# Staging q and k halves in place, one tile form for P times V, and another order of products in the middle experts of an attention, expert and gated-layer kernel

## The chip, the cores and the metric

The kernel runs on one core of a Trainium2 chip. The metric is the device time of one execution in microseconds (us), smaller is better. Times come from repeated executions; one further execution is profiled, and its trace is what the rows below are read from. The engines are TensorE (PE, with its weight loads as PEld), VectorE (DVE), ScalarE (ACT), GpSimd (POOL) and SyncE (SP), which issues most of the transfers.

## The reference

Three layers follow one another: attention with a threshold, a layer of eight experts with one expert for each token, and a gated layer.

```python
# q, k, v: (2, 8, 576, 64)
scores = scale * q @ k.T
thresh = max(scores) - tau
scores = where(scores >= thresh, scores, -1e9) - max(scores)
attn = exp(scores); attn /= sum(attn) + 1e-9
x = (attn @ v)                       # -> 1152 tokens x 512
# experts: w1 (8, 512, 1024), w2 (8, 1024, 512), capacity 288
expert_idx = argmax(x @ w_gate);  gate_w = softmax(x @ w_gate)[expert_idx]
y = relu(x_e @ w1[e]) @ w2[e]        # tokens of expert e
x = gate_w * y                       # 0 where over capacity
# gated layer: w_gate, w_val (512, 1536), w_out (1536, 512)
out = (silu(x @ w_gate) * (x @ w_val)) @ w_out
```

## The kernel before

All products keep float32 accuracy by halves: an operand is rounded to a shorter form (hi), the rest is subtracted (lo), and hi*hi + lo*hi + hi*lo are added up in PSUM.

**Attention.** Four head pairs (hp) of nine units each: four query tiles of batch 0, four of batch 1, and one unit for the tails (576 = 512 + 64). A unit (two heads) is four score products of 288 columns for the two heads (eight in the tail unit), the maximum, exponential and threshold on VectorE and ScalarE, nine transposes of the result e (L653), and, in batches, P times V (L675 for the 128-row blocks, L678 for the 64-row tail, on the V tail `vt`) and the x tasks (L709). The order on TensorE is written out by hand, by credits and by the unit numbers TST, QST and UST. Units count from 0, so hp 1 ends with unit 17 and hp 2 begins with unit 18.

The key tile KP of a head holds hi in one half of the partitions and lo in the other, so that one product multiplies both by a query tile. For each next head pair `stage_tasks` does the following: TensorE transposes raw k and q (L515), ScalarE copies the result out (L528, L530), GpSimd rounds it (L508) and subtracts (L510) on 128 partitions, which hold both heads, and SP's transfers rearrange the four quarters (head by hi or lo) into KP and the query tiles (L537 for k, L540 for q, L559 for the key tails, L568 for the query tails). Those are 28 transfers for a head pair, in the order k of batch 0, q of batch 0, tails, k of batch 1, q of batch 1.

**Experts.** Routing sorts the tokens; the experts come by size, in windows of 128, 128, 128, 144, 176, 192, 224 and 224 tokens. The first three go through `expert_rows`, which the change leaves alone. The others go through `expert`: eight h tiles (`ps_h`, first product), then four output tiles (`ps_y`, second product) of eight h tiles each. `mm_win` makes each product of two instructions: one of 2W columns (hi and lo of the tokens side by side, L1231) and one of W columns (L1232); `total` then adds the two halves of the result (a copy on ScalarE, L1240, and an addition on VectorE, L1241), and VectorE makes h's lo half (L1358). The two widest experts take their second weights in halves.

**Gated layer.** Gate and value products (L1460) and the output product (L1507 to L1509). The change leaves it alone.

## Time and profile before

| | |
|---|---|
| three runs | 566.77, 564.54, 561.7 us; median 564.54 |
| profiled execution | 564.97 us, span 563.3, mean granted clock 0.986 |
| TensorE, weight loads | 536.4 us (95%), 481.0 (85%) |
| VectorE, ScalarE | 409.7 us (73%), 295.2 (52%) |
| GpSimd | 85.4 us (15%) |
| attention | 0 to some 172 us |
| routing | 172 to 185 us |
| eight experts | 185 to 332 us |
| gated layer | 332 us to the end |

Busy time is the time in which an engine executes; weight loads run beside TensorE's products. The granted clock is the share of TensorE's full clock of 2.4 GHz that it was given, and has two levels, so a value between 0.5 and 1.0 over a stretch is a mix of 1.2 and 2.4 GHz.

### The profile page before, as it was taken

What the parts mean: (1) busy time and instruction counts of PE and PEld (TensorE: products, weight loads), DVE (VectorE), ACT (ScalarE), POOL (GpSimd) and SP (SyncE); (2) the same over time, 40 slices, a digit from 0 to 9 for tenths busy, and PEclk for the clock granted to TensorE, in tenths of its full rate; (3) what the DMA queues carried; (4) which work ended last, traced back from release to release, by engine and by line L of the source; (5) the groups of instructions that cost most, each with busy time, mean ns of one, the idle gap of its engine ahead of it and who ended that gap; (6) DMA issues with size and microseconds to landing.
All of it is one profiled execution on the core that took longest, in us unless ns stands there. A gap on an engine that the chain in (4) does not pass through costs nothing. (4 is left out here: it accounts for less than half of the span.)

```text
span 563.3 us, 9844 instructions
## 1 busy us (share of the span) xinstructions
PE 536.4 (95%) x3600; PEld 481.0 (85%) x3602; DVE 409.7 (73%) x825; ACT 295.2 (52%) x573; POOL 85.4 (15%) x145
## 2 busy tenths in 40 slices
PE   7999988999997799999999999999999999999996
PEld 6787866877773799998998889999999999888884
DVE  5988876888876399989988977888896748722220
ACT  4977664676651399877866743334332333332321
POOL 6541050055452500000000000000000000011101
PEclk8999998999999799999999999999999999999999
DMA  7557467457301888977666442442341300000001
GB/s 185 173 150 171 118 143 172 110 140 205 116 29 35 313 289 281 328 224 232 224 219 223 151 149 81 145 149 83 143 149 76 112 40 1 0 38 37 20 38 42
DMA packets 67895, 77.94 MB, mean 138 GB/s; under 512 B 25216, under 2 KB 43136, under 8 KB 67840
## 3 DMA queue, kind: packets, MB, share of 16 engines
q1 hardware_dynamic: 66256, 72.52, 42.4%
q0 software_dynamic: 1440, 4.72, 2.2%
q8 instruction: 30, 0.49, 0.3%
q14 instruction: 25, 0.20, 0.1%
q10 hardware_dynamic: 144, 0.00, 0.0%
HBM read 61.89 MB, written 4.72 MB: 118 GB/s over the span
## 5 line engine op out<-in xcount | busy, mean ns | idle before, releaser
L1460 PE MATMUL pgv<-yT,ring 128*128 128x384 f32 x828 | 145.1, 337 | 0.0
L1460 PEld LDWEIGHTS pgv<-yT,ring 128*128 128x128 f32 x828 | 144.9, 188 | 0.0
L210 ACT CAST ring<-raw 128x1024 fp32r<-128x1024 f32 x57 | 60.8, 1066 | 51.2 <-DVE raw L238 49.5
L657 ACT COPY pT<-ps_pt 128x512 f32<-128x512 f32 (+1 forms) x108 | 52.3, 486 | 41.6 <-PE ps_pt L653 41.6
L607 DVE TENSOR_REDUCE nm<-s 128x1 f32<-128x576 f32 x72 | 54.4, 755 | 17.2 <-PE s L597 17.1
L631 DVE SCALAR_TENSOR_TENSOR e<-s,th,e 128x576 f32<-128x576 f32 x72 | 58.7, 816 | 6.2 <-ACT e L620 4.9
L1513 POOL DMA_INDIRECT out_dram<-ob,ids x9 | 8.7, 972 | 358.9 <-ACT ob L1512 351.7
L620 ACT ACTIVATE e<-s,nm 128x576 f32<-128x576 f32 x72 | 54.3, 754 | 2.2 <-DVE nm L607 1.8
L288 DVE TENSOR_TENSOR ring<-raw,ring 128x1024 fp32r<-128x1024 f32 x44 | 53.3, 1218 | 0.0
L1231 PE MATMUL ps_y<-h,ring 128*128 128x448 f32 (+3 forms) x160 | 48.8, 370 | 3.6 <-DVE h L1358 3.4
L214 DVE TENSOR_TENSOR hs<-h,hs 128x768 fp32r<-128x768 f32 x18 | 17.2, 958 | 48.1 <-ACT hs L210 48.1
L653 PE MATMUL ps_pt<-ident,e 128*128 128x128 f32 x324 | 47.9, 276 | 0.0
L1231 PE MATMUL ps_h<-xw,ring 128*128 128x448 f32 (+3 forms) x160 | 46.4, 362 | 0.0
L1508 PE MATMUL po<-ring,hs 128*128 128x512 f32 x108 | 42.0, 389 | 0.0
L1507 PE MATMUL po<-ring,hs 128*128 128x512 f32 x108 | 42.0, 389 | 0.0
L1509 PE MATMUL po<-ring,hs 128*128 128x512 f32 x108 | 42.0, 389 | 0.0
L1232 PE MATMUL ps_y<-h,ring 128*128 128x224 f32 (+3 forms) x160 | 40.0, 250 | 0.0
L1232 PE MATMUL ps_h<-xw,ring 128*128 128x224 f32 (+3 forms) x160 | 40.0, 250 | 0.0
L675 PE MATMUL ps_pv<-pT,v 128*64 128x256 f32 (+2 forms) x400 | 39.9, 331 | 0.0
L653 PEld LDWEIGHTS ps_pt<-ident,e 128*128 128x128 f32 x324 | 39.7, 142 | 0.2 <-issue 0.2
L1231 PEld LDWEIGHTS ps_y<-h,ring 128*128 128x128 f32 x160 | 30.0, 188 | 8.3 <-DVE h L1358 7.4
L1480 ACT ACTIVATE sg<-pgv 128x384 f32<-128x384 f32 x36 | 17.5, 486 | 28.4 <-PE pgv L1460 18.9
(224 smaller groups left out, 975.9 us busy)
## 6 DMA issues: line engine op xcount, KB each, us to landing
raw<-in_moe_w_dram SPq DMA_DIRECT2D x25, 1024.0 KB, 5.1
rawx<-in_moe_w_dram SPq DMA_DIRECT2D x7, 1024.0 KB, 5.9
raw<-in_moe_w_gate_dram SPq DMA_DIRECT2D x6, 1024.0 KB, 5.0
qhl<-ring SPq DMA_DIRECT2D x16, 256.0 KB, 4.4
raw<-in_moe_w_out_dram SPq DMA_DIRECT2D x4, 1024.0 KB, 4.9
kp<-ring SPq DMA_DIRECT2D x24, 128.0 KB, 2.3
rawx<-in_moe_w_val_dram SPq DMA_DIRECT2D x3, 1024.0 KB, 5.0
raw<-in_moe_w_val_dram SPq DMA_DIRECT2D x3, 1024.0 KB, 5.0
```

The source lines that it names most:

```text
L210: nc.scalar.copy(dst, src)
L288: lo_eng.tensor_tensor(out=lo_, in0=src, in1=f32(hi_), op=ALU.subtract)
L607: nc.vector.tensor_reduce(out=nm_t[u][:, j:j + 1], in_=s_t[i][:, :, 0:SH], axis=AX.XY, op=ALU.max, negate=True)
L620: nc.scalar.activation(out=e_t[u][:, j].rearrange("p (a s) -> p a s", a=2), in_=s_t[i][:, :, 0:SH], func=ACTF.Exp, bias=nm_t[u][:, j:j + 1 ...
L631: nc.vector.scalar_tensor_tensor(out=ev, in0=s_t.pop(i)[:, :, 0:SH], scalar=th_t[u][:, j:j + 1], in1=ev, op0=ALU.is_ge, op1=ALU.mult, accu ...
L653: nc.tensor.transpose(ps[:, c * 128:(c + 1) * 128], ef[:, (c0 + c) * 128:(c0 + c + 1) * 128], ident)
L657: return lambda: nc.scalar.copy(pT[g][:, c0:c0 + m, o:o + 128], ps[:, 0:m * 128].rearrange("p (c t) -> p c t", c=m))
L1231: mm(ps[:, 0:2 * W], ws(wp, 0), x[:, 0:2 * W], start=first, stop=False)
L1232: mm(ps[:, 0:W], ws(wp, 1), x[:, 0:W], start=False, stop=last)
L1460: mm(ps[:, 0:TH], (gw, vw)[w][:, i, kk, fl * 128:(fl + 1) * 128], yT[:, x, kk, th * TH:(th + 1) * TH], start=i + x + kk == 0, stop=i == 1 ...
L1507: mm(po, hs[:, 0, fl], ws[:, 0, sl], start=f == 0, stop=False)
L1508: mm(po, hs[:, 0, fl], ws[:, 1, sl], start=False, stop=False)
```

## The change

- **Staging.** Each of GpSimd's operations works on the 64 partitions of one head and writes the half that is already on the right partitions straight into KP or the query tile; the other half goes there by one transfer. There are twice as many of these operations and 12 transfers for a head pair instead of 28. The order is k of batch 0, tails, q of batch 0, k of batch 1, q of batch 1; the constants TST and UST start the transposes and the staging one unit earlier. Raw k and q are loaded with one transfer for each batch instead of two, and V of the head pairs from 2 on is loaded five units later than before.
- **V tails.** Two persistent tiles, zeros outside the tail, so that the tail's product takes all 128 contraction rows.
- **Wide experts.** From 2W > 400 on (width 224), three products of W columns take the place of the two, and nothing is to be added behind them.
- **Widths 144, 176, 192.** The second product begins output tile 0 with six h tiles, then tile 1 with six, then adds the last two to each.
- Late constants are loaded at unit 11 instead of 5, a memset of the routing goes from VectorE to GpSimd, and the `olo` tiles share a buffer with the attention's e.

```diff
-    TST = 4
+    TST = 3
+    VST = 5
-    UST = 5
+    UST = 4
...
+    vtail = [ld.tile([128, B, 2, D], F32, name=f"vtail{i}") for i in range(2)]
...
         def main(nm, b, eng):
             if hp and nm != "v":
-                for h in range(2):
-                    eng.dma_start(r[nm][:, b, :, h],
-                                  srcs[nm][0][b, h0 + h, 0:SM, :].rearrange("(p c) d -> p c d", c=C4))
+                eng.dma_start(r[nm][:, b],
+                              srcs[nm][0][b, h0:h0 + 2, 0:SM, :].rearrange(
+                                  "h (p c) d -> p c h d", c=C4))
                 return
...
+        if hp < 2:
+            values()
+        else:
+            vlate[hp] = values
...
     def stage_tasks(hp):
...
-                    parts([x[:, i, cs] for i in range(2)], dst)
-                    for j in range(2):
-                        for i in range(2):
-                            to, frm = slice(i * D, (i + 1) * D), slice(j * D, (j + 1) * D)
-                            if nm == "k":
-                                o = ST if j else 0
-                                nc.sync.dma_start(f32(KP[hp, j][to, b, o:o + SM]), f32(x[frm, i, cs]))
-                            else:
-                                t = ring[3 + j] if hp % 2 == 0 else qhl[j]
-                                nc.sync.dma_start(f32(t[to, :, cs]), f32(x[frm, :, cs]))
+                    lo_, up = slice(0, D), slice(D, 2 * D)
+                    if nm == "k":
+                        k0, k1 = [KP[hp, j][:, b, o:o + SM] for j, o in ((0, 0), (1, ST))]
+                        x = kx[:, cs]
+                        rounded(k0[lo_], dst[lo_])
+                        rest_of(x[lo_], dst[lo_], k0[lo_])
+                        nc.sync.dma_start(f32(k0[up]), f32(x[lo_]))
+                        rounded(x[up], dst[up])
+                        rest_of(k1[up], dst[up], x[up])
+                        nc.sync.dma_start(f32(k1[lo_]), f32(x[up]))
+                    else:
+                        for j, frm, to in ((0, lo_, up), (1, up, lo_)):
+                            t = by_batch(ring[3 + j] if hp % 2 == 0 else qhl[j])[:, b]
+                            rounded(t[frm, 0:SM], dst[frm])
+                            rest_of(t[frm, SM:2 * SM], dst[frm], t[frm, 0:SM])
+                            nc.sync.dma_start(f32(t[to]), f32(t[frm]))
...
-        return [main("k", 0), main("q", 0), tails, main("k", 1), main("q", 1)], qtails
+        return [main("k", 0), tails, main("q", 0), main("k", 1), main("q", 1)], qtails
...
-                        mm(ps[j * D:(j + 1) * D, o:o + w], r["vt"][j * ST:(j + 1) * ST, bb, :],
-                           p[j * ST:(j + 1) * ST, C4, o:o + w], start=False, stop=True)
+                        mm(ps[j * D:(j + 1) * D, o:o + w], r["vt"][:, bb, j, :],
+                           p[:, C4, o:o + w], start=False, stop=True)
...
-            if 2 * W <= 512:
+            if 2 * W <= 400:
                 mm(ps[:, 0:2 * W], ws(wp, 0), x[:, 0:2 * W], start=first, stop=False)
                 mm(ps[:, 0:W], ws(wp, 1), x[:, 0:W], start=False, stop=last)
             else:
                 mm3(ps[:, 0:W], wp, ws, x, lambda x, i: x[:, i * W:(i + 1) * W], first, last)
...
+            def products(m, fs):
+                if fs[0] == 0:
+                    ps = ps8.tile([128, 512], F32, tag="m", name="ps_y")
+                    pys[m] = ps, pieces.pop(("w2", e, m))[:, :, :].rearrange(
+                        "p i (k f) -> p i k f", k=KF)
+                ps, wv = pys[m]
+                for f in fs:
+                    mm_win(W, ps, wv, lambda w, i: w[:, i, f], hs[f], f == 0, f == KF - 1)
+
+            head, tail_ = range(KF - 2), range(KF - 2, KF)
...
+                    if m == 0:
+                        products(0, head)
+                        products(1, head)
+                        products(0, tail_)
+                        products(1, tail_)
+                    elif m > 1:
+                        products(m, range(KF))
```

Three places in the order of instructions. First SP's queue and GpSimd around the staging for hp 2. SP before (`kp` key tiles, `ring_96` and `ring_95` scratch tiles, `thl` the tails, `ring_98` and `ring_99` query tiles, `xd` an output of the attention):

```order
L537 DMA kp_1118<-ring_96 64x512 x2
L537 DMA kp_1119<-ring_96 64x512 x2
L540 DMA ring_98<-ring_95 64x2x512 x2
L540 DMA ring_99<-ring_95 64x2x512 x2
L748 DMA xd<-xr 128x128
L748 DMA xd<-xr 128x2x128
L559 DMA kp_1118<-thl 64x2x64 x2
L559 DMA kp_1119<-thl 64x2x64 x2
```

SP after (`kth` is the scratch tile of the key tails):

```order
L557 DMA kp_1063<-ring_96 64x512
L560 DMA kp_1064<-ring_96 64x512
L586 DMA kp_1063<-kth 64x2x64
L589 DMA kp_1064<-kth 64x2x64
L775 DMA xd<-xr 128x128
L775 DMA xd<-xr 128x2x128
L337 DMA k<-in_k_dram 128x8x64
L566 DMA ring_98<-ring_98 64x1024
L566 DMA ring_99<-ring_99 64x1024
```

Four tail transfers stood behind eight others (k and q); now two tail transfers stand behind two, and each q tile takes one.

GpSimd before, from the first of these operations (`raw_103` holds transposed k and q):

```order
L508 TENSOR_SCALAR ring_96<-raw_103 128x512
L510 TENSOR_TENSOR ring_96<-raw_103,ring_96 128x512
L508 TENSOR_SCALAR ring_95<-raw_103 128x512
L510 TENSOR_TENSOR ring_95<-raw_103,ring_95 128x512
L729 TENSOR_TENSOR lg<-lt 128x24
L508 TENSOR_SCALAR thl<-traw 128x256
L510 TENSOR_TENSOR thl<-traw,thl 128x256
```

GpSimd after:

```order
L526 TENSOR_SCALAR kp_1063<-raw_103 64x512
L530 TENSOR_TENSOR ring_96<-raw_103,kp_1063 64x512
L526 TENSOR_SCALAR ring_96<-raw_103 64x512
L530 TENSOR_TENSOR kp_1064<-raw_103,ring_96 64x512
L526 TENSOR_SCALAR kp_1063<-traw 64x2x64
L530 TENSOR_TENSOR kth<-traw,kp_1063 64x128
L526 TENSOR_SCALAR kth<-traw 64x128
L530 TENSOR_TENSOR kp_1064<-traw,kth 64x2x64
L526 TENSOR_SCALAR thl<-traw 128x128
L530 TENSOR_TENSOR thl<-traw,thl 128x128
L756 TENSOR_TENSOR lg<-lt 128x24
L526 TENSOR_SCALAR ring_98<-raw_103 64x512
```

Each of the wide operations has become two on 64 partitions, and the tails stand ahead of q.

Second, TensorE in the second product of expert 3 (width 144), its first two output tiles (the numbers of h are eight h tiles, the last two of them `h_3411` and `h_3426` before, `h_3386` and `h_3401` after). Before:

```order
L1231 MATMUL ps_y_3436<-h_3393,ring1_96 128x288
L1232 MATMUL ps_y_3436<-h_3393,ring1_96 128x144
L1231 MATMUL ps_y_3436<-h_3411,ring1_96 128x288
L1232 MATMUL ps_y_3436<-h_3411,ring1_96 128x144
L1231 MATMUL ps_y_3436<-h_3426,ring1_96 128x288
L1232 MATMUL ps_y_3436<-h_3426,ring1_96 128x144
L1231 MATMUL ps_y_3494<-h_3315,ring2_97 128x288
L1232 MATMUL ps_y_3494<-h_3315,ring2_97 128x144
```

After:

```order
L1265 MATMUL ps_y_3424<-h_3353,ring2_97 128x288
L1266 MATMUL ps_y_3424<-h_3353,ring2_97 128x144
L1265 MATMUL ps_y_3424<-h_3368,ring2_97 128x288
L1266 MATMUL ps_y_3424<-h_3368,ring2_97 128x144
L1265 MATMUL ps_y_3411<-h_3386,ring1_96 128x288
L1266 MATMUL ps_y_3411<-h_3386,ring1_96 128x144
L1265 MATMUL ps_y_3411<-h_3401,ring1_96 128x288
L1266 MATMUL ps_y_3411<-h_3401,ring1_96 128x144
L1265 MATMUL ps_y_3424<-h_3386,ring2_97 128x288
L1266 MATMUL ps_y_3424<-h_3386,ring2_97 128x144
L1265 MATMUL ps_y_3424<-h_3401,ring2_97 128x288
L1266 MATMUL ps_y_3424<-h_3401,ring2_97 128x144
```


Before, the seventh and eighth h tile follow the sixth at once; after, six items of the second output tile stand between the sixth (`h_3368`) and them; the rows above begin with the last two of these.

Third, VectorE at the beginning of expert 6 (width 224). Before:

```order
L288 TENSOR_TENSOR ring_96<-raw_101,ring_96 128x1024
L1241 TENSOR_TENSOR a<-a,ps_h 128x224 x2
L1358 SCALAR_TENSOR_TENSOR h<-a,h 128x224
L288 TENSOR_TENSOR ring_97<-raw_101,ring_97 128x1024
L1241 TENSOR_TENSOR a<-a,ps_h 128x224
L1358 SCALAR_TENSOR_TENSOR h<-a,h 128x224
L1241 TENSOR_TENSOR a<-a,ps_h 128x224
L1358 SCALAR_TENSOR_TENSOR h<-a,h 128x224
```

After:

```order
L289 TENSOR_TENSOR ring_96<-raw_101,ring_96 128x1024
L1392 SCALAR_TENSOR_TENSOR h<-ps_h,h 128x224
L289 TENSOR_TENSOR ring_97<-raw_101,ring_97 128x1024
L1392 SCALAR_TENSOR_TENSOR h<-ps_h,h 128x224 x2
L289 TENSOR_TENSOR ring_98<-raw_103,ring_98 128x1024
L1392 SCALAR_TENSOR_TENSOR h<-ps_h,h 128x224 x2
L289 TENSOR_TENSOR ring_99<-raw_103,ring_99 128x1024
```

The additions L1241 are gone, and `h` is made from `ps_h` itself.

## Rows read from the trace of the kernel before

**Rows 1.** Waits of TensorE over the span: microseconds in total, times, longest.
```profile
PE ps_y L1231 <- DVE h L1358: 3.4, 5, 1.1
PE s L597 <- DMA kp<-thl: 3.4, 2, 3.1
```

**Rows 2.** Windows of units 16, 17 and 18: busy time, granted clock, DMA share.
```profile
74.60:78.86 4.26, 4.26 (x36) 3.27 (x35) 3.31 (x10) 2.60 (x5) 2.79 (x4) 1.00 0.92 215
78.86:86.75 7.89, 4.83 (x35) 3.49 (x34) 3.85 (x10) 3.37 (x7) 1.88 (x2) 0.98 0.57 124
86.75:92.55 5.80, 5.80 (x35) 4.31 (x34) 3.41 (x9) 2.98 (x6) 0.00 (x0) 0.73 0.74 170
```

**Rows 3.** Timeline of unit 17: start, duration, engine, work, idle time before.
```profile
79.73 3.23 SPq L559 DMA_DIRECT2D kp<-thl  x4
...
86.14 0.57 PE L597 MATMUL s<-kp,ring 128*128 128x288 f32 x2 [3.06 <-DMA kp<-thl]
```

**Rows 4.** Timeline: the first staging operation for head pair 2 on GpSimd.
```profile
70.07 0.62 POOL L508 TENSOR_SCALAR ring<-raw 128x512 fp32r<-128x512 f32 x1 [3.73 <-DMA qt<-thl]
```

**Rows 5.** GpSimd's groups by form: busy us, mean ns, idle before.
```profile
L510 POOL TENSOR_TENSOR ring<-raw,ring 128x512 fp32r<-128x512 f32 x12 | 15.3, 1278 | 1.0
...
L508 POOL TENSOR_SCALAR ring<-raw 128x512 fp32r<-128x512 f32 x12 | 7.4, 618 | 33.6 <-ACT raw L530 15.4 <-PE s L597 11.0 <-DMA qt<-thl 3.7
...
L510 POOL TENSOR_TENSOR thl<-traw,thl 128x256 fp32r<-128x256 f32 x3 | 2.2, 730 | 0.2
...
L508 POOL TENSOR_SCALAR thl<-traw 128x256 fp32r<-128x256 f32 x3 | 1.2, 406 | 0.1
```

**Rows 6.** DMA issues: KB each, median us from issue to landing.
```profile
ring<-ring SPq DMA_DIRECT2D x8, 256.0 KB, 4.5
```

**Rows 7.** TensorE's groups by line: busy us, mean ns.
```profile
L678 PE MATMUL ps_pv<-pT,vt 64*64 64x256 f32 (+2 forms) x100 | 13.3, 342 | 0.0
```

**Rows 8.** Timeline of TensorE in head pair 1.
```profile
51.15 1.95 PE L675 MATMUL ps_pv<-pT,v 128*64 128x256 f32 x16
...
53.03 0.79 PE L597 MATMUL s<-kp,qhl 128*128 128x288 f32 x4
...
64.41 0.65 PE L675 MATMUL ps_pv<-pT,v 128*64 128x256 f32 x4
...
64.99 0.65 PE L678 MATMUL ps_pv<-pT,vt 64*64 64x256 f32 x4
```

**Rows 9.** Windows, first and second product, widths 144 to 224 (the last: second only): busy time, granted clock, DMA.
```profile
232.47:240.48 8.01, 8.01 (x70) 8.01 (x68) 7.84 (x16) 6.04 (x17) 0.00 (x0) 1.00 0.83 300
240.48:249.81 9.33, 8.46 (x66) 7.99 (x65) 8.41 (x18) 6.54 (x15) 0.00 (x0) 1.00 0.79 245
249.81:258.57 8.76, 8.76 (x66) 8.76 (x65) 7.83 (x17) 6.95 (x17) 0.00 (x0) 1.00 0.66 210
258.57:269.13 10.56, 9.45 (x67) 8.82 (x65) 9.55 (x20) 7.00 (x16) 0.00 (x0) 1.00 0.74 252
269.13:278.41 9.28, 9.28 (x66) 9.28 (x65) 8.30 (x19) 7.61 (x19) 0.00 (x0) 1.00 0.60 197
278.41:288.73 10.32, 9.86 (x66) 9.16 (x65) 9.29 (x18) 6.70 (x14) 0.00 (x0) 1.00 0.74 238
288.73:298.77 10.04, 10.04 (x66) 9.59 (x65) 9.04 (x20) 8.33 (x19) 0.00 (x0) 1.00 0.55 198
298.77:309.68 10.91, 10.78 (x66) 9.56 (x65) 9.54 (x17) 6.84 (x15) 0.00 (x0) 1.00 0.68 226
319.71:332.02 12.31, 11.29 (x66) 9.56 (x65) 11.16 (x24) 5.76 (x14) 0.00 (x0) 1.00 0.27 83
```

**Rows 10.** Timeline of TensorE at the second product of width 144.
```profile
242.72 0.40 PE L1231 MATMUL ps_y<-h,ring 128*128 128x288 f32 x1 [0.86 <-DVE h L1358]
```

**Rows 11.** Windows in the gated layer: gate and value, output.
```profile
340.00:480.00 140.00, 140.00 (x802) 1.00 0.29 98
505.00:545.00 40.00, 40.00 (x178) 1.00 0.08 33
```

More of the change, by code (lines that the diff above doesn't have):

```diff
@@ L355, in load_qkv, with values @@
         tail("q", nc.sync)
-        for b in range(B):
-            main("v", b, nc.sync)
-        tail("v", nc.sync)
+        def values():
+            for b in range(B):
+                main("v", b, nc.sync)
+            tail("v", nc.sync)
+        if hp < 2:
+            values()
+        else:
+            vlate[hp] = values
+    vlate = {}
     def prep_tasks(hp, pick):
@@ L400, in attention_moe_swiglu_kernel, with by_batch, q_pair @@
     QH, QL, KP = {}, {}, {}
-    QT = [ld.tile([128, 2, 2 * 128], F32R, name=f"qt{j}") for j in range(2)]
-    QTH, QTL = [[QT[j][:, w] for j in range(2)] for w in range(2)]
+    QT = [ld.tile([128, 5 * 128], F32R, name=f"qt{j}") for j in range(2)]
+    QTH, QTL = [[QT[j][:, w * 384:w * 384 + 256] for j in range(2)] for w in range(2)]
     traw = ld.tile([128, 2, 128], F32, name="traw")
-    thl = ld.tile([128, 2, 2, 128], F32R, name="thl")
+    thl = ld.tile([128, 2, 128], F32R, name="thl")
+    kth = ld.tile([128, 128], F32R, name="kth")
     qhl = [ld.tile([128, 2, B * SM], F32R, name=f"qhl{j}") for j in range(2)]
     ready = set()
+    def by_batch(t):
+        return t[:, :, :].rearrange("p w n -> p (w n)").rearrange("p (b n) -> p b n", b=B)
+    def q_pair(hp, j):
+        t = by_batch(ring[3 + j] if hp % 2 == 0 else qhl[j])
+        return [t[:, :, w * SM:(w + 1) * SM] for w in range(2)]
     def tr_qk_tasks(hp):
@@ L589, in emit_qk @@
         s = sp.tile([128, 2, 512], F32, tag="s", name="s")
-        col = (b * C4 + c) * 128
         if b >= 0:
-            jobs = [(QH[hp, j][:, col:col + 128], b), (QL[hp, j][:, col:col + 128], b)]
+            jobs = [(Q[hp, j][:, b, c * 128:(c + 1) * 128], b) for Q in (QH, QL)]
         else:
@@ L778, in attention_moe_swiglu_kernel @@
     keep_warm(mp, WARM0, 128)
+    for vz in vtail:
+        nc.vector.memset(vz, 0.0)
     nc.scalar.dma_start(tau_sb, tau.partition_broadcast(128))
@@ L938, in attention_moe_swiglu_kernel @@
             qtails()
+        if live and st == VST and hp + 1 in vlate:
+            assert not any(g[0] < hp for _, _, g in pvq)
+            vlate.pop(hp + 1)()
     assert not trq
@@ L1072, in rhs_op @@
                         in1=tokf[:, :, i].unsqueeze(2).to_broadcast([128, NTL, NTL]), op=ALU.mult)
-    olo = [rp.tile([128, 128], BF16, name=f"olo{t}") for t in range(NTL)]
+    olo_all = ep.tile([128, 2, S], F32, tag="e", name="olo")[:, :, :].rearrange(
+        "p j s -> p (j s)").bitcast(BF16)
+    olo = [olo_all[:, t * 128:(t + 1) * 128] for t in range(NTL)]
     sq = [rp.tile([128, 128], BF16, name=f"sq{i}") for i in range(len(AOLO))]
@@ L1216, in rest @@
         sort_scale(NS0 + 1)
-        V.memset(xsT[:, :, NT:], 0.0)
+        nc.gpsimd.memset(xsT[:, :, NT:], 0.0)
         def window(e):
@@ L1236, in total @@
         def total(W, ps):
-            if 2 * W > 512:
+            if 2 * W > 400:
                 return ps[:, 0:W]
@@ L1386, in expert @@
                         next_piece()
+            pys = {}
+            def products(m, fs):
[7 more added lines that the diff above has]
+            head, tail_ = range(KF - 2), range(KF - 2, KF)
             for m in range(KD):
-                ps = ps8.tile([128, 512], F32, tag="m", name="ps_y")
                 if e in halves:
+                    ps = ps8.tile([128, 512], F32, tag="m", name="ps_y")
                     for f in range(KF):
@@ L1395, in expert @@
                 else:
-                    wp = pieces.pop(("w2", e, m))
-                    wv = wp[:, :, :].rearrange("p i (k f) -> p i k f", k=KF)
-                    for f in range(KF):
-                        mm_win(W, ps, wv, lambda w, i: w[:, i, f], hs[f], f == 0, f == KF - 1)
+                    if m == 0:
[5 more added lines that the diff above has]
+                        products(m, range(KF))
+                    ps = pys[m][0]
                 if e == 0:
```

63 lines of the change are left out of this document (33 added, 30 removed).

## The prediction

> **What bounds the kernel now.** I read the page's first part, then the waits, then windows and timelines of the stages that the diff touches. TensorE is busy for 95% of the span, and the table of waits holds only some 20 us in all; two rows of it lie in touched code [rows 1]. The first is that of the second expert product, 3.4 us on h tiles; the second that of the attention's scores on the key's halves, 3.4 us in two waits, one of 3.06. So a gain comes out of these waits, out of TensorE's own instructions, or not at all. The other engines have slack: GpSimd, on which the staging of the next head pair runs, is busy for 15%.
>
> **A. Staging of the next head pair.** Unit 17, the last of head pair 1, takes 7.89 us where unit 16 takes 4.26; unit 18 then runs 5.80 us at a granted clock of 0.73, so part of it is at the 1.2 GHz level, after a stretch in which TensorE stood still [rows 2]. The timeline names the cause: the four key-tail transfers of L559 are issued at 79.73 and take 3.23 us, behind the other transfers of the SP queue; TensorE has nothing more at 83.08 and goes on at 86.14, 3.06 us later, released by the tail [rows 3].
>
> The change begins the staging one unit earlier, puts the tails second in the order (before: third), and sends 12 transfers for each pair instead of 28. Before, GpSimd's first rounding starts at 70.07 [rows 4]. One unit (some 4.2 us [rows 2]) earlier is 65.9. The new work of GpSimd: a tile of 512 columns was rounded and subtracted on 128 partitions in 0.62 + 1.28 = 1.9 us [rows 5]; now there are two such pairs on 64 partitions each. No row shows an operation of 64 partitions; the nearest is the same shape on 128. The bounds are 0.95 us (time follows the elements) and 2.5 us (a third more for another access); I take 1.9, the row of the same width.
>
> The Trainium skill speaks against the change here. The rows give 1.9 us for 128 partitions and nothing for 64. "GPSIMD Engine Reference", Architecture, says that each of its cores works on its own sixteen partitions; by it half of the cores idle in the new operations and nothing is saved by the smaller tile. No run here shows it so far; by it the sum stays as it is, and by the lower bound it would be earlier still.
>
> So k of batch 0 takes 3.8 us, the tails three pairs of 128 columns. From 512 and 256 columns (618 and 406 ns, 1278 and 730 ns) [rows 5] 128 columns would take 0.30 + 0.46 us, three pairs 2.3; the bounds are 1.4 (a quarter of the wide pair, three times) and 5.7 (three full pairs). Then q of batch 0, 3.8. Sum: 65.9 + 3.8 + 2.3 + 3.8 = 75.8; the q transfer lands some 4.5 us after its issue [rows 6], at 80.3. TensorE asks at about 83.1: a margin of 2.8 us. Key and tail are then long there.
>
> Gain: the wait of 3.06 [rows 1, 3], the other one of about 0.4 (of 3.4 us, two times), and what unit 18 lost to the clock: 5.80 - 4.26 = 1.54. Together **-5.0 us**. Bounds: -3.5 (the clock falls there for another reason) to -5.6 (some short waits of the first unit go too); the row of the clock stands right behind the wait, so I keep it in. The transposes of the staging move from unit to unit and stay equal in number. What is late next is the softmax chain on VectorE, which a unit without waits keeps at 3.3 of 4.26 us [rows 2]. The late V loads, the moved constants, the memset that goes to GpSimd and the new place of the olo tiles I cost at nothing: they are transfers or short operations of engines with slack under TensorE's stream. If that cover were gone, one V load that a unit waits for would cost about what a transfer of its 256 KB takes to land, 4.5 us [rows 6].
>
> **B. The tail of P times V.** Before, it has 64 contraction rows in a 64*64 tile (L678), in the middle of items of 128*64 (L675). Its 25 items (x100, four instructions each [rows 7]) make 31 changes of tile form inside runs of such items (19 into L678, 12 back), counted along TensorE's timeline. What a change costs: four items of one form take 1.88 us from 51.15 to 53.03, while a single item that is followed by another form takes 0.58 (64.41 to 64.99) [rows 8]. So an item in form takes (1.88 - 0.58) / 3 = 0.43, and a change costs 0.15. In the new kernel all items have the 128*64 form, with a V tail padded by zeros to 128 rows: 31 x 0.15 = 4.65 us of TensorE's time. Not all of it reaches the end, as in head pair 0 and where VectorE sets the pace TensorE only waits longer. I take 0.7 of it: **-3.2 us**, bounds 0 and -4.6. The memsets of the padding run at the start, under the first loads.
>
> **C. Six h tiles first, widths 144, 176, 192.** Their second product takes 9.33, 10.56 and 10.32 us, their first one 8.01, 8.76 and 9.28 with as many products [rows 9]: the second loses 1.32 + 1.80 + 1.04 = 4.16 us. The new order has twelve items (six of each of two output tiles) before the seventh h tile is asked for. But the timeline shows the first wait, 0.86 us, at the sixth h tile: five pairs run from the stage's start at 240.48, and the sixth begins at 242.72 [rows 9, 10]. It lies within the new head, so it stays. What can go is what the seventh and eighth tile wait after it, some quarter of the loss: **-1.0 us**, bounds 0 and -4.2. No product is added.
>
> **D. The two experts of width 224.** Before, a pair of a 448-column and a 224-column product; now three of 224 columns, and no copy (ScalarE) and addition (VectorE) behind them. Their second products lose 10.91 - 10.04 = 0.87 and 12.31 - 10.04 = 2.27 us to the first one [rows 9] (that of the last expert is as long). Without the addition the last h tile is ready earlier; I take 2.6 of these 3.14 as gone. TensorE's own cost: 140 us hold 802 products of 384 columns, 174.6 ns each; 40 us hold 178 of 512, 224.7 ns [rows 11]: 0.39 ns a column. So 448 columns take 200 ns, and the pair's measured 10.04 us / 32 = 314 ns [rows 9] leave 114 for the narrow one. Three are 342 instead of 314, or 336 with the 112 by columns: 25 ns more, times 2 experts x 64 pairs = 128: **+3.2 us**. Bounds: 100 ns for each narrow product (-1.8 us) and 125 (+7.8), which is what a product of the narrowest expert takes on the mean, 8.01 us / 64 [rows 9]. I take the middle one, out of rows of the same tiles.
>
> The row leaves 114 ns for a product of 224 columns. "TensorE: Matmul & The Clock Gate", LDWEIGHTS, gives a load of 128 weight columns as 128/1.2 = 107 ns, and a product can't follow faster than its weights. By it three take 320 ns and part D's own cost is +0.9 us in place of +3.2, so that the sum would be lower by 2.3. The sum goes by the row.
>
> **Sum.** -5.0 - 3.2 - 1.0 - 2.6 + 3.2 = -8.6 against the profiled execution of 564.97 us (span 563.3 and 1.7 around it), which stands 0.4 above the median of 564.54. That is 556.4; against the median 555.9. **I predict 556.**
>
> **Rivals.**
> - *The narrow products eat it.* Each takes 125 ns instead of 114 (+4.6 us), and the tile changes of B lay beside VectorE's work, so that of B only 0.5 comes through (+2.7): 556 + 7.3 = 563.3. For it: the expert of width 144 does take 125 ns on the mean; VectorE is busy for 7.84 of 8.01 us there [rows 9]. Against it: it is VectorE that would set that pace, and the new form takes work from it.
> - *The stall only moves.* The last thing that the first unit of a head pair needs is then the q half instead of the key tail, and TensorE waits as long as now: 556 + 5 = 561. For it: the q transfers are the slowest of the staging, 4.5 us. Against it: the margin of 2.8 us.
> - *Slower: GpSimd's doubled queue.* GpSimd has twice as many operations for k and q. If a half takes more than 2.5 us, the four halves and the tails ahead of the q transfer cost 4 x 0.6 = 2.4 us more, and with a tail at 5.7 (+3.4) the margin of 2.8 is gone. At 3.2 a half all three boundaries of head pairs wait, each 3.1 us and 1.5 for the clock: 3 x 4.6 = 14 us in place of the 5 gained, 556 + 14 = 570. It decides from 2.5 us for a half on. Against it: the row for the same width on 128 partitions.
>
> **How the numbers follow.** Forecast 0.71, with its own range 551 to 559.5 (A to -5.6, B to -4.6, C to -2, D's cost to +0.9 below; B to -1.5, D to +5 above). Narrow products 0.13, stall moves 0.10, slower queue 0.06. The range reaches from the forecast's lower end to 561.5, over the moved stall: left out are most of the first rival, the slower queue and some 0.04 below, together not quite 0.2. One per cent is about what a measurement of this kernel tells from no change: under 558.9 is faster, which is 0.68 (the forecast without its upper end); within 1% are that end and two rivals, 0.26; slower 0.06.
>
> **What the profile of the changed kernel would show.** A: the wait of the scores on kp is gone from the table of waits, unit 17 takes 4.3 to 4.9 us, and the granted clock of unit 18 is near 1.00; GpSimd's 64-partition operations take 0.62 and 1.28 us. B: no 64*64 products; items of P times V at 0.43 us also where the tail stands among them. C: second products of widths 144 to 192 of some 9.0, 10.1 and 10.1 us, with the wait on the sixth h tile still there. D: first products of width 224 of 10.8 us in place of 10.04, with second ones close to them. The prediction is wrong if the wait comes back under the name of a q tile, if a narrow product costs 125 ns, or if an attention unit doesn't get shorter where its tile changes went.

## The result and the profile after

The changed kernel takes 559.26 us in the median of 15 runs (557.28 to 563.9), the kernel before 565.61 (15 runs): a ratio of 0.9898, 95% interval 0.9876 to 0.992, or 5.8 us less (the two medians alone are 6.4 apart). The profiled execution has a span of 559.8 us, so it shows 3.5 us of that. The first part of its page:

```profile
PE 531.5 (95%) x3730; PEld 486.4 (87%) x3730; DVE 403.0 (72%) x802; ACT 287.9 (51%) x549; POOL 115.0 (21%) x188
```

TensorE is still busy for 95%; GpSimd went from 15 to 21%, VectorE from 409.7 to 403.0 us. The waits of TensorE that answer to [rows 1] (microseconds in total, times, longest):

```profile
PE ps_g L1221 <- DMA raw<-xd,ids: 7.0, 1, 7.0
PE ps_y L1265 <- DVE h L1392: 4.4, 5, 1.1
```

The wait on a key tail is gone. That on h tiles, which the change was to shorten by its order of products, grew: at widths 144 to 192 from 2.4 us in three waits to 4.4 in five (the other 1.0 of the 3.4 before lay at width 224 and is gone). A wait of 7.0 us on gathered rows stands first, where the kernel before had 3.3. Units 17 and 18, which answer to [rows 2]:

```profile
81.00:86.28 5.28, 5.28 (x43) 4.58 (x42) 4.57 (x12) 2.88 (x6) 4.86 (x6) 1.00 0.37 99
86.28:89.70 3.42, 3.42 (x30) 2.43 (x29) 3.23 (x8) 2.62 (x6) 1.60 (x4) 1.00 0.70 146
```

Units 17 and 18 take 8.70 us in place of 13.69, both at full clock. GpSimd's new operations, by form (busy us, mean ns), which answer to [rows 5]:

```profile
L530 POOL TENSOR_TENSOR kp<-raw,ring 64x512 fp32r<-64x512 f32 x6 | 7.7, 1282 | 0.5
...
L526 POOL TENSOR_SCALAR ring<-raw 64x512 fp32r<-64x512 f32 x10 | 6.2, 617 | 0.8
```

On 64 partitions they take what they took on 128, 0.62 and 1.28 us: nothing is saved by the smaller tile. The Trainium skill says that each of GpSimd's cores works on its own sixteen partitions ("GPSIMD Engine Reference", Architecture); the trace agrees with what the prediction drew from it. The second products of widths 144, 176 and 192, then the first product of the first expert of width 224 and the second product of the last; they answer to [rows 9]:

```profile
237.00:245.92 8.92, 8.05 (x66) 7.88 (x65) 7.41 (x16) 5.20 (x13) 0.00 (x0) 1.00 0.67 211
254.68:266.10 11.42, 9.43 (x66) 8.80 (x65) 9.40 (x19) 7.09 (x18) 0.00 (x0) 1.00 0.63 190
275.39:286.81 11.42, 9.86 (x67) 9.16 (x65) 9.37 (x18) 6.74 (x18) 0.00 (x0) 1.00 0.64 195
286.81:297.54 10.73, 10.73 (x98) 10.73 (x97) 9.80 (x16) 8.64 (x18) 0.00 (x0) 1.00 0.69 237
318.98:329.70 10.72, 10.72 (x98) 10.72 (x97) 7.01 (x12) 3.50 (x7) 0.00 (x0) 1.00 0.24 73
```

Width 144 gained 0.41 us, 176 and 192 lost 0.86 and 1.10. At 224 first and second products are alike at 10.7: no wait is left there.

One statement ahead of the prediction is wrong: the two experts of width 224 don't take their second weights in halves, so that the new order of products holds for them too, not for widths 144 to 192 alone.

### The profile page after: what moved, and what is told of

Same layout as the page of the kernel before. It is cut to its first block, busy times and chain, and to the rows that moved or that the text cites. A ratio compares the mean times of both kernels' runs of the same rounds, so it can differ in the third digit from the quotient of the medians.

```text
span 559.8 us, 10018 instructions
## 1 busy us (share of the span) xinstructions
PE 531.5 (95%) x3730; PEld 486.4 (87%) x3730; DVE 403.0 (72%) x802; ACT 287.9 (51%) x549; POOL 115.0 (21%) x188
## 3 DMA queue, kind: packets, MB, share of 16 engines
q0 software_dynamic: 1440, 4.72, 2.1%
HBM read 61.89 MB, written 4.72 MB: 119 GB/s over the span
## 5 line engine op out<-in xcount | busy, mean ns | idle before, releaser
L1531 DVE TENSOR_TENSOR h<-sg,pgv 128x384 f32<-128x384 f32 x36 | 19.7, 548 | 17.6 <-PE pgv L1510 17.2
L1265 PE MATMUL ps_y<-h,ring 128*128 128x288 f32 (+2 forms) x96 | 27.0, 357 | 4.4 <-DVE h L1392 4.4
L211 ACT CAST ring<-rawx 128x1024 fp32r<-128x1024 f32 x19 | 20.1, 1067 | 21.6 <-DVE rawx L239 21.5
L702 PEld LDWEIGHTS ps_pv<-pT,v 128*64 128x64 f32 x400 | 21.6, 136 | 10.7 <-issue 4.2
L624 PE MATMUL s<-kp,ring 128*128 128x288 f32 x128 | 26.8, 337 | 1.3 <-DVE th L642 0.7
```

The lines of the kernel that those rows point to most:

```text
L211: nc.scalar.copy(dst, src)
L702: mm(ps[j * D:(j + 1) * D, o:o + w], r["v"][:, bb, j, c, :], p[:, j * (C4 + 1) + c, o:o + w], start=c == 0, stop=False)
```

## The experiments

Of four parts (staging, V tail, order of products, narrow products) each was undone or made alone. The smaller changes (loads, late constants, memset, the place of `olo`) were undone in no run but the one with narrow products alone; elsewhere they stay with the staging. Each ratio is to runs of the kernel before that were made beside it. A difference in us between two kernels is the difference of their ratios, times 566 us. Four groups of runs share their runs of the kernel before: from the base to the order undone, from the later start to staging and tail alone, from narrow products alone to width 192, and staging alone; across groups a difference is less sure. A base run and eleven others:

**The changed kernel again.**

> The changed kernel once more, as the base of this group of runs and for a second profile. Ratio to before near 0.990. The first profile of it shows 2.8 us lost in head pair 0 (the first two units run at granted clocks of 0.50 and 0.73, before at 0.95 and 1.00) and 3.7 us lost in the routing (TensorE waits 7.0 us for the first gathered rows, before 3.3, behind a gather that GpSimd begins 2.5 us after its indices, before 1.1). Theory chance: both differ between executions, and one or both are gone here. Theory program: both come from the changed program's instructions and are here again, within 0.5 us.

Measured: 0.9883 (0.9857 to 0.9908). Head pair 0's first two units run at full clock here (6.92 us as in the kernel before, against 8.61), so that loss was chance. From the last index product of the routing to the first product on gathered rows (`ps_g`), 9.6 us in the first profile, 7.0 is left; before it was 5.9. Head pair 0's units 2 to 8 are as long as in the first profile (28.4 us; before 27.5): that is the program's.

**V tail undone.**

```diff
-   mm(..., r["vt"][:, bb, j, :], p[:, C4, o:o + w], ...)
+   mm(..., r["vt"][j * ST:(j + 1) * ST, bb, j, :], p[j * ST:(j + 1) * ST, C4, o:o + w], ...)
```

> Undoes the V tail alone: the tail's product takes its 64 rows in a 64*64 tile again. Theory of the prediction: 31 changes of the tile form at 0.15 us come back, of which 0.7 reach the end: 3.2 us more than the changed kernel, and units of head pairs 1 to 3 longer by 0.1 to 0.3 each where a change was. Rival: VectorE sets the pace there and the changes are hidden: within 0.5 us of the changed kernel.

Measured: 0.9957 (0.9936 to 0.9977), 4.2 us more than the base. Units 2 to 8, 9 to 16, 17 and 18, 19 to 25, 27 to 34, first of the base:

```profile
17.98:46.38 28.40, 27.72 (x221) 22.66 (x220) 24.08 (x60) 23.18 (x51) 18.98 (x54) 1.00 0.51 142
46.38:79.14 32.76, 31.21 (x274) 25.76 (x273) 28.47 (x72) 23.68 (x50) 15.26 (x27) 1.00 0.50 111
79.14:87.79 8.65, 8.65 (x70) 6.97 (x69) 7.75 (x20) 5.49 (x11) 6.40 (x9) 1.00 0.49 111
87.79:116.60 28.81, 28.17 (x251) 23.41 (x250) 24.98 (x62) 21.16 (x45) 12.57 (x20) 1.00 0.40 99
121.60:154.82 33.22, 32.92 (x287) 26.72 (x286) 30.83 (x82) 21.96 (x46) 22.45 (x23) 1.00 0.36 108
```

then of this run:

```profile
19.88:48.93 29.05, 28.23 (x218) 22.30 (x219) 24.26 (x61) 23.21 (x51) 17.91 (x48) 1.00 0.45 128
48.93:82.33 33.40, 32.20 (x273) 25.57 (x273) 28.72 (x72) 23.75 (x50) 15.06 (x27) 1.00 0.50 111
82.33:91.28 8.95, 8.95 (x70) 6.79 (x69) 7.61 (x21) 5.50 (x11) 6.08 (x8) 1.00 0.55 123
91.28:121.14 29.86, 29.22 (x251) 23.21 (x250) 25.13 (x60) 21.40 (x45) 12.97 (x21) 1.00 0.37 91
126.21:160.19 33.98, 33.97 (x286) 26.29 (x286) 30.91 (x82) 21.82 (x46) 21.90 (x23) 1.00 0.35 103
```

All are longer, by 0.65, 0.64, 0.30, 1.05 and 0.76 us; with unit 26 (0.07) and the products after the last unit (10.35 against 9.16) that makes 4.66. It looks like the whole of the prediction's 31 x 0.15 = 4.65, but that is chance: counted along TensorE's timeline in the same way, this run has 38 changes of the tile form (24 into the tail, 14 back) where the kernel before has 31, as has the run with the staging alone: the new staging shifts the items on TensorE. The price holds. Item by item against the base, where the same items follow one another, a change into the tail costs 0.10 us, one back 0.15, and the item behind 0.05 more, 5.7 us in all, or 38 x 0.15. Of it 4.66, or 0.82, stands in the stages. Units 2 to 8, 17 and 18, 19 to 25 and the products after the last unit lose nearly what their 4, 2, 8 and 8 changes cost (0.65, 0.30, 1.05 and 1.19 of 0.6, 0.3, 1.2 and 1.2); units 9 to 16 and 27 to 34, with 7 and 9 changes, hide some 40% (0.64 of 1.05, 0.76 of 1.35).

**Narrow products undone.**

```diff
-            if 2 * W <= 400:
+            if 2 * W <= 512:
...
-            if 2 * W > 400:
+            if 2 * W > 512:
```

> Undoes the three narrow products alone: the two experts of width 224 take the 448 and 224 column pair, the copy and the addition again. Theory now, from the profile of the changed kernel: 1.5 us more than the changed kernel (first products 10.04 instead of 10.74 each, second ones some 0.2 and 1.6 longer, and 1.2 more ahead of the gate products, since the last output waits for an addition). The prediction's own balance: 0.6 us less than the changed kernel (the narrow products cost 3.2 and give back 2.6).

Measured: 1.0019 (1.0006 to 1.0033), 7.7 us more than the base, five times what was expected. The two second products of width 224 and the stretch behind them:

```profile
293.31:305.37 12.06, 10.81 (x67) 9.57 (x65) 9.65 (x19) 7.00 (x17) 0.00 (x0) 1.00 0.60 194
315.39:328.72 13.33, 10.91 (x66) 9.57 (x65) 11.72 (x24) 6.46 (x17) 0.00 (x0) 1.00 0.23 78
328.72:340.00 11.28, 9.69 (x44) 8.82 (x43) 6.62 (x12) 5.15 (x11) 0.00 (x0) 0.85 0.49 172
```

They take 12.06 and 13.33 us (10.91 and 12.31 before the change), and at the start of the gated layer TensorE waits 1.6 us for an output and the granted clock falls to 0.85; from the first gate product to the first output product it takes 155.2 us in place of 151.2. With the order of products the two-instruction form is worse than it was without.

**Order of products undone.**

```diff
                     if m == 0:
-                        products(0, head)
-                        products(1, head)
-                        products(0, tail_)
-                        products(1, tail_)
-                    elif m > 1:
+                        products(0, range(KF))
+                    else:
                         products(m, range(KF))
```

> Undoes the order of products alone: each output tile takes its eight h tiles one after the other. The prediction: 1.0 us more than the changed kernel. Theory now: VectorE, with ScalarE in lock step, is what these stages wait for (h tiles and weight preparation), and another order of TensorE's products takes no work from it; the three experts take 56.3 us again in place of 57.8, so 1.5 us less than the changed kernel. If VectorE's backlog is simply kept, the first waits after the change of expert are as long in either order.

Measured: 0.9827 (0.9807 to 0.9847), 555.93 us: 3.2 us less than the base, the lowest ratio of the study. Its second products of widths 144, 176 and 192:

```profile
232.79:242.12 9.33, 8.46 (x67) 7.99 (x65) 8.41 (x18) 6.55 (x15) 0.00 (x0) 1.00 0.79 254
250.88:261.41 10.53, 9.44 (x67) 8.82 (x65) 9.53 (x20) 6.98 (x16) 0.00 (x0) 1.00 0.74 256
270.69:281.00 10.31, 9.85 (x66) 9.16 (x65) 9.28 (x18) 6.69 (x14) 0.00 (x0) 1.00 0.69 245
```

They are those of the kernel before to 0.03 us. So the order costs 1.6 us in the profile at these widths (31.76 against 30.17); the rest of the 3.2 lies within the two intervals. The waits of ScalarE and VectorE between 229 and 287 us of the changed kernel show why:

```profile
ACT a L1274 <- PE ps_y L1266: 3.7, 3, 1.3
DVE a L1275 <- ACT a L1274: 3.0, 3, 1.1
```

and of the kernel before in its same stage (no such row of VectorE stands there):

```profile
ACT a L1240 <- PE ps_y L1232: 0.2, 1, 0.2
```

With six and six the first output tile is complete after fourteen pairs in place of eight. ScalarE, and VectorE behind it, stand still for 1.0 to 1.3 us in each of the three experts, and then have two output tiles at once, with the next expert's h tiles queued behind these. The end of width 144 on VectorE (L1456) and TensorE's waits in the second product of width 176, in the changed kernel:

```profile
250.23 0.31 DVE L1456 TENSOR_TENSOR yT<-a,yT 128x144 f32 x1 [0.38 <-ACT yT L1455]
...
256.52 0.43 PE L1265 MATMUL ps_y<-h,ring 128*128 128x352 f32 x1 [0.86 <-DVE h L1392]
...
258.66 0.43 PE L1265 MATMUL ps_y<-h,ring 128*128 128x352 f32 x1 [1.13 <-DVE h L1392]
```

and in the kernel before:

```profile
252.78 0.31 DVE L1406 TENSOR_TENSOR yT<-a,yT 128x144 f32 x1 [0.38 <-ACT yT L1405]
...
261.22 0.43 PE L1231 MATMUL ps_y<-h,ring 128*128 128x352 f32 x1 [1.11 <-DVE h L1358]
```

The last output of width 144 leaves VectorE 4.62 us after the next expert's first product has begun (245.92), before 3.28 (249.81). In that next expert TensorE then waits for the fourth and for the sixth h tile, before for the sixth alone, and both lie in the head of six, where the order can't help; width 192 does the same. Width 144 has the new order too, but the expert ahead of it is one that the change left alone: it waits for the sixth h tile as before, and it gained 0.41 us. So the order gains a little in its own expert and loses more in the one that follows. This chain is read from the timelines; no run changes one link of it by itself.

**Staging begun one unit later** (TST = 4 and UST = 5).

> The changed kernel with the staging begun one unit later, as before the change; its order and its 12 transfers stay. Theory: the earlier start is what took the wait at the boundaries of head pairs away, and it costs head pair 0 (units 2 to 8 take 28.4 us in place of 27.5). Then GpSimd is done with q of batch 0 some 4.2 us later, a wait of 1.5 to 3 us comes back at the first unit of head pair 2 under the name of a q tile, the clock falls after it again, and head pair 0 gets 1 us back: 1 to 4 us more than the changed kernel in all. Rival: fewer transfers and tails ahead of q are enough by themselves: no wait, and 1 to 1.6 us less than the changed kernel.

Measured: 0.994 (0.9919 to 0.996), 3.2 us more than the base. Units 17 and 18:

```profile
78.44:83.52 5.08, 4.55 (x35) 3.40 (x34) 3.92 (x11) 3.38 (x7) 4.58 (x7) 1.00 0.69 154
83.52:87.70 4.18, 4.18 (x35) 3.15 (x34) 3.46 (x8) 2.88 (x6) 3.93 (x5) 1.00 0.48 118
```

Against the base unit 18 loses 0.8 us and unit 27 1.1, units 8 and 9 together 1.3; the table of waits has q tiles for it now (0.8 on a transfer, 0.5 on GpSimd). Units 17 and 18 still take 9.26 us and not 13.69, so the start is worth some 1 us for each boundary and not the whole wait. Another 1.8 us goes at unit 29 (unit 30 gives 1.0 of it back), where a VectorE operation on six columns, elsewhere 0.2 us long, runs beside one of GpSimd and ends with it:

```profile
132.88 2.38 POOL L289 TENSOR_TENSOR ring<-raw,ring 128x1024 fp32r<-128x1024 f32 x1
...
133.31 1.97 DVE L724 TENSOR_SCALAR rinv<-ssum 128x6 f32<-128x6 f32 x1
```

**Tails third in the staging again.**

```diff
-        return [main("k", 0), tails, main("q", 0), main("k", 1), main("q", 1)], qtails
+        return [main("k", 0), main("q", 0), tails, main("k", 1), main("q", 1)], qtails
```

> The changed kernel with the tails third in the staging again, behind q of batch 0. Theory: GpSimd has the same work ahead of the first unit of the next head pair in either order, so units 17 and 18 stay within 0.3 us of 5.2 and 3.4, and the time is that of the changed kernel within 1 us. Rival: the order removed the wait, which then comes back on the tail (up to 3 us at unit 18).

Measured: 0.9891 (0.9853 to 0.9928), units 17 and 18 at 5.01 and 3.67 us: the order of the staging is worth nothing that can be told. Both runs kept the 12 transfers; a run with 28 transfers and the new start was not made, so that the transfers' share is what is left over, not measured by itself. The timelines show where it lies. In the kernel before, GpSimd was done with the key tails at 75.38 us, but they stood in SP's queue until 79.73 [rows 3] and were out at 82.96, behind four k and four q transfers; the k ones alone:

```profile
70.72 3.11 SPq L537 DMA_DIRECT2D kp<-ring  x4
```

With the staging one unit later GpSimd is done with them at 75.51, much as before, and they are out at 75.94; with the tails third, at 76.15. So the tails are out some 7 us earlier in the run without the early start, and no later in the one without the new order: what is left is the shorter queue, with the later loads, which both runs had too.

**Places in GpSimd's instruction stream.** On top of the run with the order undone:

```diff
     credit, xn = 0, []
+    shift = ld.tile([128, 1], F32, name="shift")
+    for _ in range(24):
+        nc.gpsimd.memset(shift, 0.0)
```

> The changed kernel with each output tile's eight h tiles one after the other, and 24 memsets of one column on GpSimd ahead of the attention's loop, which change nothing but the places in GpSimd's instruction stream. In five runs of changed kernels an instruction transfer comes 0.6 us behind the first olo operation on GpSimd, and the first gather begins 1.7 to 2.5 us after its indices; in the kernel before the transfer comes 6.5 us ahead of olo and the gather after 1.1 us. Theory: the gather waits for GpSimd's instructions; shifted, that transfer comes earlier, the gather begins after 1.1 us, and the time from the last index product to the first gate product falls from 6.5 (the same kernel without the memsets) or more to 5.9. Rival: the transfer belongs to another engine, or the delay to something else: gather delay of 1.7 to 2.5 us as now.

Measured: 0.9853 (0.9823 to 0.9883), the same as without within the intervals. The instruction transfer 0.6 us behind `olo` (an operation of the routing) is gone, the last one ahead of the gather comes 6 us before `olo`, and the gather begins 2.0 us after its indices, as in the other changed kernels. My theory falls. What the gather's first wait follows is the landing of the attention's last rows, two transfers of 32.2 KB: 3.3 us after their issue in the first profile of the kernel before, 3.8, 3.9 and 4.5 in the base, this run and the first profile of the changed kernel, and the gather begins 1.1, 1.9 to 2.0 and 2.5 us after its indices.

**Staging and tail alone** (both edits above that undo the experts' parts).

> Staging and V tail alone: the experts are as before the change (448 and 224 column pair with addition, eight h tiles in a row). Theory, the parts depend on each other in the experts: here the two widest experts take 43.3 us as before, not 45.5 as with the order of products and no narrow products, and the start of the gated layer loses 1.2 us and not 4.0: 565.9 - 3.4 (staging) - 4.2 (tail) + some 1.5 (later gather) = 560, ratio 0.989 to 0.991. Rival, the parts add up: the order costs 2.7 and the narrow products gain 7.7 in the changed kernel, so without both 558.3 - 2.7 + 7.7 = 563.3, ratio 0.995.

Measured: 0.9872 (0.9844 to 0.99). The parts in the experts depend on each other, and more than expected: without both, the kernel is about as fast as with both.

**Narrow products alone** (the kernel before, 2W > 400).

> The kernel before with the three narrow products at width 224 as its only change. Theory: VectorE and ScalarE are what the widest experts wait for, so the part gains by itself about what it gains beside staging and tail: 3.1 us of waits in the second products and 1.2 ahead of the gate products for 2.7 us of TensorE's time, and a shorter chain at the end of the experts, 1.5 to 2.5 us less than before, ratio 0.9955 to 0.997. Rival (the prediction's own balance of that part): 0.6 us more than before. The profile is also a second one of the routing of the kernel before: theory program, the last attention rows land 3.3 us after their issue and the first gather begins 1.1 us after its indices, as in the first profile; theory chance, 3.6 to 4.5 and 1.6 to 2.5 as in the changed kernels.

Measured: 0.9976 (0.9957 to 0.9996), 1.4 us less. The part gains by itself, where the prediction's balance had a loss. The profile also settles the gather: with the routing of the kernel before, the last rows land after 4.1 us and the gather begins 1.8 us after its indices. What the first two profiles showed there was chance: the time from the last index product to the first product on gathered rows is 5.9 and 9.6 us in them and 6.4 to 8.0 in the twelve others.

**GpSimd for a third of the weights' lo halves at widths 144 to 192** (on top of the run with the order undone).

```diff
-            lo_eng = lo_eng or nc.vector
+            lo_eng = lo_eng or (nc.gpsimd if pool_lo and used["piece"] % 3 == 0 else nc.vector)
```

> The changed kernel with eight h tiles in a row, and GpSimd makes every third lo half of the expert weights at widths 144 to 192 (8 subtractions of 2.4 us there in place of 8 of 1.2 us on VectorE). Theory: the second products of these widths wait for VectorE's queue, so taking 3.3 us from it in each expert takes most of the 4.1 us of waits away: second products within 0.5 us of the first ones (8.0, 8.8, 9.3), 2.5 to 4 us less than the same kernel without (0.983), ratio 0.976 to 0.979. Rival: the waits come from the chain of an h tile itself (product, copy, addition, halves), which the weights don't touch: second products stay at 9.3, 10.5 and 10.3. Second rival: two engines on one memory slow each other, and VectorE's operations grow.

Measured: 0.9938 (0.992 to 0.9957), 6 us more than without (5 by the run with memsets, the same kernel otherwise). The second rival it is. In the timeline at the end of width 144's first product, VectorE's operation on an h tile (L1394) takes 0.31 us, then beside GpSimd's subtraction 2.23:

```profile
233.16 0.31 DVE L1394 SCALAR_TENSOR_TENSOR h<-a,h 128x144 fp32r<-128x144 f32 x1
...
234.15 2.65 POOL L290 TENSOR_TENSOR ring<-raw,ring 128x1024 fp32r<-128x1024 f32 x1 [48.68 <-ACT ring L211]
...
234.73 2.23 DVE L1394 SCALAR_TENSOR_TENSOR h<-a,h 128x144 fp32r<-128x144 f32 x1
...
237.02 0.40 PE L1266 MATMUL ps_y<-h,ring 128*128 128x288 f32 x1 [2.79 <-DVE h L1394]
```

It ends 0.16 us after GpSimd's, and TensorE waits 2.79 us. Seven of the eight subtractions hold one VectorE operation so, by 1.5 to 2.2 us, and the eighth costs 0.6: 13 us in all. The additions that take one input from PSUM (L1276) run beside them unchanged, in 0.30 to 0.35 us. The Trainium skill says it ("GPSIMD Engine Reference", Specifications: the two engines contend for SBUF where VectorE's instruction has two inputs there or is in a mode of two ports). The trace agrees for the operations with two inputs; one of those held is a cast with one input (2.83 us in place of 0.62), whose mode no run shows. So whether VectorE's load is the cause of the 4.2 us of waits was not tested by this run.

**Narrow products at width 192 too** (2W > 370, on top of the run with the order undone).

> The changed kernel with eight h tiles in a row and the three narrow products at width 192 as well. Theory: at 224 columns a narrow product took 112 ns; at 192 it can't fall under what a product of 144 columns in the narrowest expert leaves it, so three take 310 to 330 ns for a pair's 290, 1.3 to 2.6 us more for the expert, and the copies and additions that go take its wait of 1.0 us and part of the wait of 224 (none is left there): 0.3 to 1.6 us more than the same kernel without. Rival: relief of VectorE counts more, also for the expert behind: 1 us less.

Measured: 0.9884 (0.9859 to 0.9909), 3.2 us more than without (1.8 by the run with memsets). First and second product of width 192:

```profile
261.77:272.50 10.73, 10.73 (x98) 10.73 (x97) 8.81 (x16) 7.62 (x15) 0.00 (x0) 1.00 0.73 230
272.50:283.22 10.72, 10.72 (x98) 10.72 (x97) 7.50 (x10) 5.07 (x8) 0.00 (x0) 1.00 0.56 190
```

Each takes 10.73 us, as at 224 columns. A narrow product costs 112 ns (10.73 / 96) at either width: it isn't paid by its columns, and TensorE's weight loads fill the whole stretch (10.73 us). The Trainium skill's 107 ns for a load of 128 weight columns ("TensorE: Matmul & The Clock Gate", LDWEIGHTS) is near it, and the measurement decides: 112. The expert takes 21.45 us in place of 19.60: three narrow products cost more than the wait of 1.0 us that went, and at 224 no wait was left to go.

**Staging alone.**

> Staging alone: the changed kernel with the tail's product on 64 rows in a 64*64 tile, the 448 and 224 column pair and eight h tiles in a row. Theory, staging and tail add up in the attention: by stages of the profiles staging gives 7 us back at the boundary to head pair 2 or somewhat more, and costs 1.6 in head pair 0 and 0.7 in pair 2; with staging and tail at 0.987 and the tail at 4.2 to 4.7 us, staging alone is 2.9 to 3.4 us less than before, ratio 0.994 to 0.995. Rival: the tail's gain needs the shorter waits of the staging, or the other way round, and staging alone gives over 5 us or under 1.

Measured: 0.9969 (0.995 to 0.9987), 1.8 us less than before. By the same five groups of units as above:

```profile
17.24:46.25 29.01, 28.33 (x221) 22.29 (x220) 24.28 (x60) 23.20 (x51) 20.25 (x57) 1.00 0.54 149
46.25:79.63 33.38, 32.19 (x274) 25.56 (x273) 28.71 (x72) 23.70 (x50) 15.05 (x27) 1.00 0.50 109
79.63:88.60 8.97, 8.97 (x70) 6.80 (x69) 7.61 (x20) 5.48 (x11) 6.08 (x8) 1.00 0.57 128
88.60:118.43 29.83, 29.19 (x251) 23.18 (x250) 25.12 (x60) 21.37 (x45) 12.95 (x21) 1.00 0.38 92
123.57:157.47 33.90, 33.89 (x286) 26.21 (x284) 30.91 (x81) 21.70 (x46) 21.87 (x23) 1.00 0.36 104
```

Before, they were 27.46, 33.39, 13.69, 29.12 and 35.10 us long. The boundary to head pair 2 gives 4.72 us, and pair 3 1.20; pair 0 costs 1.55 and units 19 to 25 0.71. That is 3.7 us by stages, more than the ratio's interval allows (0.7 to 2.8): the profiled execution, at 561.42 us, is the fastest of twelve with a median of 564.78, and where the others lose the rest is not shown. Staging that begins earlier moves other work of TensorE ahead too: in pair 0 it is busy for 28.33 us where it was 26.24, in pair 3 for 33.89 where it was 35.10. In pair 0 that work falls into units that VectorE paced; units 5 and 6 went from 3.42 and 3.47 to 4.24 and 4.12 with this tail, 4.12 each with the new one.

All ratios to the kernel before:

| staging | tail | narrow | order | ratio | interval |
|---|---|---|---|---|---|
| x | | | | 0.9969 | 0.995 to 0.9987 |
| | | x | | 0.9976 | 0.9957 to 0.9996 |
| x | x | | | 0.9872 | 0.9844 to 0.99 |
| x | x | x | | 0.9827 | 0.9807 to 0.9847 |
| x | x | | x | 1.0019 | 1.0006 to 1.0033 |
| x | | x | x | 0.9957 | 0.9936 to 0.9977 |
| x | x | x | x | 0.9898 | 0.9876 to 0.992 |
| x | x | x | x | 0.9883 (base run) | 0.9857 to 0.9908 |
| x | x | x | | 0.9853 (24 memsets more) | 0.9823 to 0.9883 |

## Why the prediction was right, and where its steps were not

The time lies 3.3 us above the forecast of 556 and within the range; 1.1 of the 3.3 is the kernel before, whose fifteen runs have a median of 565.61 where the first three had 564.54. By the ratio it is 1.0% faster, on the very border between the forecast's two classes. But the sum came out by errors that cancel, and that is luck. Against the -8.6 us of the working the ratios give -5.8; the parts, priced one by one, make -5.3.

- **A, staging: -5.0 forecast, -1.8 measured** (interval -2.8 to -0.7). The mechanism was right where it was read: the wait on the tail went, the clock of unit 18 stayed at 1.00, and units 17 and 18 gave 4.7 to 5.0 us. GpSimd's 0.62 and 1.28 us held. The step that failed is the sentence that the transposes move and stay equal in number, costed at nothing: moving TensorE's work into units with no room cost 1.55 us in head pair 0 and 0.7 in units 19 to 25, of which pair 3 gave 1.2 back. And the early start that the working rested on is worth some 1 us a boundary, not 4; by the timelines the shorter queue of SP did the rest, which no run has by itself. How much A is worth stays open between 1.8 us by its own ratio, 3.0 (staging and tail together, less the tail's 4.2) and 3.7 by stages; a second profile of the old attention (narrow products alone) has 15.36 us for units 17 and 18 in place of 13.69, so that the wait itself differs between executions.
- **B, tail: -3.2 forecast, -4.2 measured, 4.66 by stages.** The price of 0.15 us a change held. The term that was mis-sized is the count: 31 in the kernel before, 38 with the new staging, 5.7 us in all. Of these 0.82 (by stages) or 0.74 (by ratios) reach the end, near the 0.7 that was taken.
- **C, order: -1.0 forecast, +3.2 measured** (+1.6 in the profile at widths 144 to 192). The step that failed is the view behind "No product is added", that only TensorE's waits on the seventh and eighth h tile change. The evacuation of the first output tile is put off by six pairs, the two engines that evacuate stand idle until then, and the next expert's fourth and sixth h tiles come later. Where no such expert stands ahead (width 144) the order gave 0.41 us, as the working would have it.
- **D, narrow products: +0.6 net forecast, -1.4 alone, -2.5 beside staging and tail** (-1.1 by the run with memsets, and the intervals overlap). TensorE's own cost was sized nearly right: 10.72 - 10.04 for 32 pairs and four such stages, 2.7 us for the 3.2 forecast, and 112 ns a product for 114. The working's other value, 112 by columns, hit it by luck: at 192 columns the same line (0.39 ns a column) would give 99.5, and the product takes 112 there too. What went was more than the 2.6 of waits: all 3.14, and 1.16 in the gate products (152.38 to 151.22 us), whose first ones wait for the last output; the working had not looked there.

C and D don't add up: the order costs 3.2 us with narrow products and 8.3 without (1.0019 against 0.9872), and the copy and addition that narrow products save lie on the engines that the order leaves idle and then loads at once; that this is why is the reading that fits, not tested apart. Of the rivals none came true as told: narrow products took 112 ns, not 125; no wait returned at the boundary with the early start; GpSimd's halves took 1.9 us, far from 2.5.

## What to carry to other kernels

Where two engines evacuate what a third computes, ask first whose queue ends last: an order that gives the third engine more to do before a wait can put off the first finished tile and starve the other two. A change that moves work must be priced where it arrives, not only where it leaves. Price the parts of a change one by one, but test in pairs those that load the same engine.

## What the runs showed of the hardware

- A VectorE operation of 0.3 us took 2.23 beside a GpSimd subtraction of 2.65 and ended 0.16 us after it; one of 0.2 us took 1.97 beside one of 2.38. Additions with one input in PSUM stayed at 0.30 to 0.35.
- A change of the tile form cost 0.10 us into the 64-row tail and 0.15 out of it, and 0.05 at the item behind; 38 such changes cost 4.66 us in the stages.
- Three products of 192 and of 224 columns cost the same, 112 ns each.
- Executions differ by up to 1.7 us in when TensorE's clock rises in head pair 0: the first two units took 8.61 us at granted clocks of 0.50 and 0.73, or 6.92 at 0.95 and 1.00.
- A transfer of 32.2 KB landed 3.3 to 4.5 us after its issue at one and the same place, and the gather that reads it began 1.1 to 2.5 us after its indices.
